# Places of their own for the first four steps of an attention and SoLU kernel, and two buffers for the keys

## The chip, the cores and the metric

One core of a Trainium2 chip. Its engines each run their own instructions in order: PE (TensorE, matrix products), DVE (VectorE), ACT (ScalarE), POOL (GpSimd), and SP (SyncE), which here only issues DMAs. The metric is the device time of one execution in microseconds (us); lower is better.

## What is computed

```python
scores = scale * np.matmul(q, k.transpose(0, 1, 3, 2))      # q, k, v: (8, 8, 576, 64)
kth = np.partition(scores, -32, axis=-1)[..., -32:-31]
scores = np.where(scores >= kth, scores, -1e9)
attn = np.exp(scores - scores.max(-1, keepdims=True))
attn = attn / (attn.sum(-1, keepdims=True) + 1e-09)
x = np.matmul(attn, v)                  # then heads side by side: (4608, 512)

h = x @ w_in                            # (4608, 1024)
solu = h * softmax(h)
ln = (solu - mean) / np.sqrt(var + 1e-06) * g_ln
out = ln @ w_out                        # (4608, 512)
```

The weights w_in and w_out come as 64-bit floats and are turned into 32-bit ones on the chip.

## The kernel before

**Work.** The 8 batches have 8 heads each, taken as 4 pairs of heads. A *step* is one of 32 equal pieces of the attention: four chunks of 128 queries, two from each of two head pairs, and one set of 64 last queries of one pair. With two heads per chunk that gives nine score tiles of 128 x 576 per step (`NT` = 9, index j). Four steps make a batch. After a half of a batch has its attention output (xT), the tokens pass the second part in groups of 128 (*token groups*: mm1, hexp, solu, square, ln, transposes, mm2, store), 36 groups in all.

**What one step does**, with the engine. SP loads the queries (`load_q`, L739), and for each head pair the keys with the last 64 queries and keys (`load_k`, L653) and the values (`load_v`). PE transposes queries (`prep_q`), keys (`prep_k`) and the last rows (`prep_t`); ACT copies them out of PSUM (`prep_qc`, `prep_kc`, `prep_tc`). PE forms products of keys with keys (`moments`, copied by `moments_c`); `spread` (PE), `spread_v`, `spread_r` (DVE), `first_p` (POOL) and `first` (DVE) make from them a first guess of each row's threshold. PE makes the scores (`scores`, L844, two tiles per call), ACT takes them to SBUF as X (`evac`). Then the threshold is refined: `count0` (DVE) counts entries above the first guess, `second` moves the guess, `count1` (seven tiles on ACT, two on DVE) and `third` refine it, `count2` (ACT) gives signs, `side`, `nearest`, `best` and `kth` (DVE) find the 32nd value. `exps` (ACT), `keep` and `inverse` (DVE) and `norm` (POOL) make probabilities, which PE transposes (`transpose_p`), ACT copies (`copy_p`), and PE multiplies with the values (`attn_v`, copied by `copy_v`).

**Weights.** 16 chunks of 128 x 512, w_in in chunks 0 to 7 and w_out in 8 to 15. Each is loaded (`load_w`) and converted by `w_bits` (three DVE instructions, L589, L593, L597), `w_low` (ACT, L605), `w_mul` and `w_add` (POOL, L629, L632); w_out also gets `w_gain`. At the end all chunks are read once more (`w_again`, `w_exp`, `w_check`) for a check of their range.

**Order.** It is written out by hand. Each call is put on a list with a planned time (`at`, L1173), from tables: `step_times` for a step (times from the step's own start, steps 39 apart), `key_times` for the four head pairs of a batch, `first_times` for the four token groups of the first batch, `token_times` and `tails_times` for the others, `last_times` for the last three, `weights_times` for the weights. The list is sorted by time and issued:

```python
    with tc.manual_schedule(engines={E.PE, E.Activation, E.DVE, E.Pool}):
        for _, _, f, args in sorted(todo, key=lambda x: x[:2]):
            f(*args)
```

So the planned times only make an order on PE, ACT, DVE and POOL; each instruction still waits for its data. SP is not in that set: its DMAs are put in order when the program is built, and each waits until its buffer is free.

**Buffers.** Pools `p1`, `p2`, `small`, `p8` hold 1, 2, 3 and 8 buffers of each tag. Keys (`km`, L658), the last queries and keys (`qt`, `kt`) and the step's queries (`qm`) have one buffer, raw weights two, X eight of two tiles each. In PSUM there are two buffers each for the scores (shared with `spread` and mm1), for transposes, and for the outputs (shared with `moments` and `prep_t`).

Of the kernel before, what the change touches and what calls it, by code (L numbers as in the profile page):

```python
# [15 lines left out]
P = 128  # L16
# [427 lines left out]
def fast_path(  # L444
# [23 lines left out]

    nc = tc.nc
# [3 lines left out]
    NM = 4  # L473
# [26 lines left out]

    pairs = [(b, hp) for b in range(B) for hp in range(NP)]
    steps = []
    for b in range(B):
        for half in range(2):
            for n in range(NP // 2):
                two = (2 * n + half, 2 * n + 1 - half)
                chunks = [(hp, 2 * half + t) for hp in two for t in range(2)]
                steps.append((b, chunks, two[0]))
# [144 lines left out]
    def load_k(n):  # L653
        b, hp = pairs[n]
        hh = slice(2 * hp, 2 * hp + 2)
        d = ks[n]

        d["k"] = p1.tile([P, 2 * NM, D], F32, tag="km", name="km")  # L658
        nc.sync.dma_start(
            out=d["k"].rearrange("p (t h) d -> p t h d", h=2),  # L660
            in_=k[b, hh, 0:SM, :].rearrange("h (p t) d -> p t h d", t=NM),
        )
        for nm, src in (("q", q), ("k", k)):
            d[nm + "t"] = p1.tile([ST, 2, D], F32, tag=nm + "t", name=nm + "t")
            nc.sync.dma_start(out=d[nm + "t"], in_=src[b, hh, SM:S, :].rearrange("h p d -> p h d"))
# [73 lines left out]
    def load_q(i):  # L739
        b, chunks, x = steps[i]  # L740
        d = st[i]
        d["q"] = p1.tile([P, NT, D], F32, tag="qm", name="qm")
        for c, (hp, t) in enumerate(chunks):
            nc.sync.dma_start(
                out=d["q"][:, 2 * c : 2 * c + 2, :],
                in_=q[b, 2 * hp : 2 * hp + 2, 0:SM, :].rearrange("h (p t) d -> p t h d", t=NM)[
                    :, t, :, :
                ],
            )
        for h in range(2):  # L750
            nc.sync.dma_start(
                out=d["q"][h * ST : (h + 1) * ST, 2 * NM, :], in_=q[b, 2 * x + h, SM:S, :]
            )

    def keys_of(i, c):

        b, chunks, x = steps[i]
        return ks[NP * b + (x if c == NM else chunks[c][0])]
# [217 lines left out]
    def kth(i):  # L976

        d = st[i]
        far = d["far"]
        hot = small.tile([P, NT, 8], F32, tag="hot", name="hot")  # L980
        nc.vector.tensor_tensor(
            out=hot, in0=ranks, in1=far.unsqueeze(2).broadcast_to([P, NT, 8]), op=ALU.is_equal
        )
        nc.vector.tensor_tensor(out=hot, in0=hot, in1=d["w8"].rearrange("p (t e) -> p t e", e=8), op=ALU.mult)
        zk = zk_all[:, i, :]
        nc.vector.tensor_reduce(out=zk, in_=hot, axis=AX.X, op=ALU.add)
        kt = small.tile([P, NT], F32, tag="kth", name="kth")
        nc.vector.tensor_tensor(out=kt, in0=d["al"], in1=zk, op=ALU.subtract)
        nc.vector.scalar_tensor_tensor(
            out=kt, in0=kt, scalar=-1.0, in1=kt, op0=ALU.mult, op1=ALU.max  # L990
        )
        d["kth"] = kt
# [72 lines left out]

    def attn_v(i, part):
        o = st[i]["om", part] = ps_o.tile([P, 512], F32, tag="o", name="om")
        n = 2 * P if part else SP
        vm, vt = keys_of(i, 2 * part)["v"]
        pt = pt_of(i, part)[:, :, 0:n]  # L1070

        for c in range(NM + 1):
            for h in range(2):
                hd = slice(h * ST, (h + 1) * ST)
                nc.tensor.matmul(  # L1075
                    out=o[h * D : (h + 1) * D, 0:n],
                    lhsT=vm[:, h, c, :] if c < NM else vt[hd, :],
                    rhs=pt[:, h * NM + c, :] if c < NM else pt[hd, 2 * NM, :],
                    start=(c == 0), stop=(c == NM),
                )  # L1080

    def copy_v(i, part):
        b, chunks, x = steps[i]
        hp, t = chunks[2 * part]
        o = st[i]["om", part]
        m = once(xs, ("m", b, t // 2), lambda: p2.tile([P, NP, 2 * P], F32, tag="xTm", name="xTm"))
        nc.scalar.copy(out=m[:, hp, :], in_=o[:, 0 : 2 * P])  # L1087
        if part == 0:
            m = once(xs, ("t", b // 2), lambda: p2.tile([P, NP, 2 * ST], F32, tag="xTt", name="xTt"))
            c = b % 2 * ST  # L1090
            nc.scalar.copy(out=m[:, hp, c : c + ST], in_=o[:, 2 * P : SP])
# [81 lines left out]
    def at(time, f, *args):  # L1173
# [38 lines left out]

    key_times = [
        (load_k, [-71.77, -54.35, -34.54, -26.23]),
        (load_v, [46.71, 33.98, 89.74, 55.28]),
        (prep_t, [-50.7, -40.81, -7.18, 29.61]),
        (prep_tc, [-44.69, -33.63, -1.87, 33.99]),
        (prep_k, [-57.81, -29.05, -14.02, 12.97]),
        (prep_kc, [-52.21, -21.98, -13.67, 19.04]),
        (moments, [-60.64, -32.24, -4.08, 14.96]),  # L1220
        (moments_c, [-42.18, -31.04, 2.87, 15.92]),
# [4 lines left out]
            (mm1, range(2), [55.33, 58.94]),  # L1226
            (hexp, [()], [62.09]),
            (solu, [()], [64.78]),
            (square, [()], [72.74]),
            (ln, [()], [74.12]),  # L1230
            (transpose_ln, range(2), [79.17, 82.08]),
            (copy_ln, range(2), [80.82, 83.25]),
            (mm2, range(2), [105.32, 109.34]),
            (store, [()], [116.42]),
        ],
        [
            (mm1, range(2), [56.02, 57.57]),
            (hexp, [()], [62.06]),
            (solu, [()], [63.63]),
            (square, [()], [64.41]),  # L1240
            (ln, [()], [70.76]),
            (transpose_ln, range(2), [71.53, 73.02]),
            (copy_ln, range(2), [73.11, 76.23]),
            (mm2, range(2), [103.2, 105.01]),
            (store, [()], [111.83]),
        ],
        [
            (mm1, range(2), [60.01, 58.42]),
            (hexp, [()], [60.84]),
            (solu, [()], [63.82]),  # L1250
            (square, [()], [66.16]),
            (ln, [()], [68.8]),
            (transpose_ln, range(2), [73.91, 72.15]),
            (copy_ln, range(2), [76.72, 73.77]),
            (mm2, range(2), [104.21, 109.94]),
            (store, [()], [122.21]),
        ],
        [
            (mm1, range(2), [56.27, 58.65]),
            (hexp, [()], [60.21]),  # L1260
            (solu, [()], [62.66]),
            (square, [()], [65]),
            (ln, [()], [71.02]),
            (transpose_ln, range(2), [72.95, 75.51]),
            (copy_ln, range(2), [75.72, 78.13]),
            (mm2, range(2), [100.81, 108.54]),
            (store, [()], [114.07]),
# [25 lines left out]
        (mm1, range(2), [67.83, 66.88]),  # L1293
        (hexp, [()], [71.58]),
        (solu, [()], [78.17]),
        (square, [()], [78.26]),
        (ln, [()], [85.86]),
        (transpose_ln, range(2), [91.97, 93.22]),
        (copy_ln, range(2), [93.92, 104.78]),
        (mm2, range(2), [103.52, 117.24]),  # L1300
        (store, [()], [177.72]),
# [4 lines left out]
            -179.04, -126.3, -52.39, -38.25, -33.45, 2.48, 8.22, 5.52, 52.89, 51.11, 62.18,  # L1306
            83.53, 63.6, 105.69, 111.2, 108.65,
        ]),
        (w_bits, w_wide, range(NW), [
            -155, -52.03, -42.38, -5.42, 15.63, 19.48, 57.75, 77.84, 84.56, 85.78, 92.26,  # L1310
            104.44, 115.57, 124.08, 129.87, 135.07,
        ]),
        (w_low, w_wide, range(NW), [
            -109.8, -76.02, -28.31, 1.47, 11.32, 38.79, 64.91, 76.6, 83.01, 89.83, 92.36,
            105.31, 118.79, 123.48, 128.94, 132.88,
        ]),
        (w_mul, w_wide, range(NW), [
            -73.72, -18.25, -6.71, 5.55, 20.66, 39.9, 66.53, 78.79, 93.74, 96.71, 105.83,
            111.35, 121.8, 126.63, 134.57, 135.6,
        ]),  # L1320
        (w_add, w_wide, range(NW), [
            -33.83, -13.24, 1.26, 14.88, 23.19, 58.85, 72.52, 85.73, 95.1, 99.85, 106.84,
            115.23, 122.2, 127.79, 135.39, 137.44,
        ]),
        (w_gain, True, range(8, NW), [
            113.17, 161.51, 144.58, 163.9, 157.15, 174.79, 165.41, 184.77,
        ]),
        (w_again, w_wide, range(NW), [
            1258.52, 1267.59, 1233.32, 1272.03, 1265.86, 1232.82, 1276.98, 1238.37, 1336.4,
            1328.98, 1268.82, 1395.91, 1275.47, 1295.42, 1317.39, 1347.09,  # L1330
        ]),
        (w_exp, w_wide, range(NW), [
            1333.3, 1343.97, 1271.41, 1284.48, 1356.37, 1274.22, 1344.94, 1304.11, 1362.07,
            1390.72, 1361.14, 1452.18, 1376.66, 1376.2, 1365.1, 1423.75,
        ]),
        (w_check, w_wide, range(NW), [
            1340.79, 1345.85, 1277.65, 1332.62, 1371.59, 1301.74, 1366.88, 1327.12, 1416.86,
            1444.15, 1370.39, 1493.58, 1432.99, 1419.36, 1417.83, 1433.7,
        ]),
    ]  # L1340

    at(-287.72, load_g)
    for f, needed, chunks, times in weights_times:
        for n, time in zip(chunks, times):
            if needed:
                at(time, f, n)
# [6 lines left out]
    for i in range(NSTEP):  # L1353
        all_times(i * STEP, step_times, i)
    for n in range(len(pairs)):
        for f, times in key_times:
            at(n // NP * NP * STEP + times[n % NP], f, n)
# [94 lines left out]
```

## Time and profile before

| | |
|---|---|
| median of 3 runs | 1300.66 us (1299.98 to 1301.05) |
| the profiled execution | 1299.98 us |
| its span, first to last instruction | 1298.1 us |
| busy: PE, DVE, ACT, POOL | 1194.8, 1154.8, 1118.8, 479.6 us |
| mean granted TensorE clock | 0.963 |
| 16 DMA engines, share of the span | 16% |

Busy time is the sum over an engine's instructions; with shares of 92, 89 and 86% no engine stands out, so the question is where in the span each is idle. In the lines shown later, a row of a timeline begins with its start and its duration in us, then engine, line of the kernel, operation, output tile and inputs, and in brackets the idle time of the engine before it and what ended it. A row of stretches begins with the stretch and its length, then the busy time of PE, of PE's weight loads, of DVE, ACT and POOL (number of instructions in brackets), the granted clock (1.00 is full), the mean busy share of the DMA engines, and GB/s.

### The profile page before, as it was taken

What the parts mean: (1) busy time and instruction counts of PE and PEld (TensorE: products, weight loads), DVE (VectorE), ACT (ScalarE), POOL (GpSimd) and SP (SyncE); (2) the same over time, 40 slices, a digit from 0 to 9 for tenths busy, and PEclk for the clock granted to TensorE, in tenths of its full rate; (3) what the DMA queues carried; (4) which work ended last, traced back from release to release, by engine and by line L of the source; (5) the groups of instructions that cost most, each with busy time, mean ns of one, the idle gap of its engine ahead of it and who ended that gap; (6) DMA issues with size and microseconds to landing.
All of it is one profiled execution on the core that took longest, in us unless ns stands there. A gap on an engine that the chain in (4) does not pass through costs nothing.

```text
span 1298.1 us, 20306 instructions
## 1 busy us (share of the span) xinstructions
PE 1194.8 (92%) x6243; PEld 658.0 (51%) x6243; DVE 1154.8 (89%) x2974; ACT 1118.8 (86%) x2446; POOL 479.6 (37%) x583
## 2 busy tenths in 40 slices
PE   5645879999999999999999999999999999998996
PEld 3323445555555555555555555555555555554543
DVE  4899999999999997999999997999999997999612
ACT  3787889999999889999999889999999889999534
POOL 4244654443333234443333244443333234443310
PEclk9666889999999999999999999999999999999999
DMA  6212211101110111101210112111210111102421
GB/s 163 81 43 61 67 38 28 37 22 37 46 36 17 30 32 50 34 23 31 54 36 18 30 30 54 28 29 30 55 35 19 31 28 43 30 9 73 130 73 44
DMA packets 106246, 57.00 MB, mean 44 GB/s; under 512 B 89224, under 2 KB 97424, under 8 KB 106128
## 3 DMA queue, kind: packets, MB, share of 16 engines
q1 hardware_dynamic: 106128, 55.61, 15.7%
q8 instruction: 52, 0.85, 0.3%
q14 instruction: 66, 0.54, 0.1%
HBM read 46.14 MB, written 9.44 MB: 43 GB/s over the span
## 4 chain that ended last, share of the span: by engine, by line
PE 59%; ACT 18%; DVE 15%; issue 3%; POOL 3%; DMA 1%; SPq 0%; DVEq 0%; POOLq 0%; ACTq 0%
PE o_ps L1157 15%; PE s_ps L858 12%; PE h_ps L1099 12%; PE tp_p L1026 7%; PE om L1075 7%; DVE junkv L875 4%; ACT junka L897 4%; DVE E L997 3%; ACT sg L932 3%; ACT PT L1038 2%; PE tp_ln L1146 2%; ACT E L968 2%; DVE w L953 2%; DVE w L960 2%; ACT X L867 2%
## 5 line engine op out<-in xcount | busy, mean ns | idle before, releaser
L1157 PE MATMUL o_ps<-w_out,lnT 128*128 128x512 f32 x576 | 261.8, 598 | 0.2 <-ACT osb L1164 0.2
L875 DVE TENSOR_SCALAR_CACHE_REDUCE junkv<-X,t 128x576 bf16<-128x576 f32 x288 | 230.7, 801 | 11.9 <-ACT X L867 7.3
L1012 POOL TENSOR_SCALAR E<-E,rden 128x576 f32<-128x576 f32 x256 | 204.7, 813 | 87.0 <-DVE rden L1008 76.5
L925 POOL TENSOR_SCALAR tt<-t 128x9 f32<-128x9 f32 x32 | 21.8, 680 | 573.3 <-DVE t L919 573.3
L1099 PE MATMUL h_ps<-w_in,xTm 128*128 128x512 f32 x512 | 226.7, 595 | 0.3 <-ACT xTm L1087 0.3
L953 DVE SCALAR_TENSOR_TENSOR w<-X,al,sg 128x576 f32<-128x576 f32 x256 | 210.6, 824 | 0.1
L960 DVE MAX8 w<-w 128x8 f32<-128x576 f32 x288 | 210.5, 749 | 0.0
L997 DVE SCALAR_TENSOR_TENSOR E<-X,kth,E 128x576 f32<-128x576 f32 x256 | 200.0, 818 | 9.7 <-ACT E L968 9.6
L858 PE MATMUL s_ps<-kT,qT 64*128 64x288 f32 x1024 | 195.7, 458 | 5.5 <-ACT X L867 4.5
L932 ACT ACTIVATE sg<-X,t 128x576 bf16<-128x576 f32 x256 | 195.6, 768 | 2.8 <-DVE t L919 2.8
L897 ACT ACTIVATE junka<-X,t 128x576 bf16<-128x576 f32 x224 | 174.3, 778 | 19.4 <-DVE t L888 15.6
L867 ACT ACTIVATE X<-s_ps 128x576 f32<-128x576 f32 x256 | 157.2, 655 | 36.0 <-PE s_ps L858 32.4
L1026 PE MATMUL tp_p<-ident,E 128*128 128x128 f32 x1024 | 155.5, 285 | 26.4 <-POOL E L1012 21.6
L1026 PEld LDWEIGHTS tp_p<-ident,E 128*128 128x128 f32 x1024 | 116.0, 144 | 92.9 <-issue 37.5
L1038 ACT COPY PT<-tp_p 128x512 f32<-128x512 f32 x256 | 145.6, 595 | 19.5 <-PE tp_p L1026 19.3
L1157 PEld LDWEIGHTS o_ps<-w_out,lnT 128*128 128x128 f32 x576 | 104.3, 190 | 110.6 <-issue 107.8
L1099 PEld LDWEIGHTS h_ps<-w_in,xTm 128*128 128x128 f32 x512 | 94.6, 190 | 109.7 <-issue 102.4
L968 ACT ACTIVATE E<-X 128x1152 f32<-128x1152 f32 x128 | 146.5, 1174 | 0.0
L1075 PE MATMUL om<-PT,vm 128*64 128x256 f32 (+1 forms) x1024 | 140.0, 416 | 0.0
L858 PEld LDWEIGHTS s_ps<-kT,qT 64*128 64x128 f32 x1024 | 116.2, 199 | 46.7 <-ACT X L867 18.1
L1075 PEld LDWEIGHTS om<-PT,vm 128*64 128x64 f32 x1024 | 68.5, 138 | 59.7 <-issue 22.5
L818 POOL TENSOR_TENSOR zs<-zs,phalf 128x9 f32<-128x9 f32 x32 | 70.2, 2194 | 2.7
(127 smaller groups left out, 1631.8 us busy)
## 6 DMA issues: line engine op xcount, KB each, us to landing
km<-in_k_dram SPq DMA_DIRECT2D x32, 256.0 KB, 3.3
qm<-in_q_dram SPq DMA_DIRECT2D x128, 64.0 KB, 2.1
vm<-in_v_dram SPq DMA_DIRECT2D x32, 256.0 KB, 2.8
out_dram<-osb SPq DMA_DIRECT2D x32, 256.0 KB, 2.3
w_raw<-in_moe_w_in_dram SPq DMA_DIRECT2D x8, 512.0 KB, 4.4
w_raw<-in_moe_w_out_dram SPq DMA_DIRECT2D x8, 512.0 KB, 3.3
w_again<-in_moe_w_in_dram SPq DMA_DIRECT2D x8, 512.0 KB, 4.6
w_again<-in_moe_w_out_dram SPq DMA_DIRECT2D x8, 512.0 KB, 4.1
```

The costliest lines, as they stand in the source:

```text
L858: nc.tensor.matmul(out=s[:, half, 0:SH], lhsT=queries_of(i, t)[hd, :], rhs=kT[hd, k0 : k0 + SH], start=True, stop=True,)
L875: nc.vector.tensor_scalar(out=junk, in0=x_of(i, j), scalar1=st[i][t][:, j : j + 1], scalar2=None, op0=ALU.is_ge, op1=ALU.add, accum_out=co ...
L897: nc.scalar.activation(out=junk, in_=x_of(i, j), func=AF.Sign, scale=-1.0, bias=d["t1"][:, j : j + 1], accum_out=columns(i, "n1")[:, j : j ...
L932: nc.scalar.activation(out=d["sg", j], in_=x_of(i, j), func=AF.Sign, scale=-(1.0 + 2.0**-23), bias=d["t2"][:, j : j + 1], accum_out=column ...
L953: nc.vector.scalar_tensor_tensor(out=w, in0=x_of(i, j), scalar=d["al"][:, j : j + 1], in1=d.pop(("sg", j)), op0=ALU.subtract, op1=ALU.mult,)
L960: nc.vector.max(w8[:, j, :], st[i].pop(("w", j)))
L997: nc.vector.scalar_tensor_tensor(out=e, in0=x_of(i, j), scalar=d["kth"][:, j : j + 1], in1=e, op0=ALU.is_ge, op1=ALU.mult, accum_out=den_a ...
L1012: nc.gpsimd.tensor_scalar(out=e, in0=e, scalar1=st[i]["rden"][:, j : j + 1], scalar2=1.0, op0=ALU.mult, op1=ALU.mult,)
L1026: nc.tensor.transpose(tp[:, c, :], e[:, c * P : (c + 1) * P], ident)
L1075: nc.tensor.matmul(out=o[h * D : (h + 1) * D, 0:n], lhsT=vm[:, h, c, :] if c < NM else vt[hd, :], rhs=pt[:, h * NM + c, :] if c < NM else ...
L1099: nc.tensor.matmul(out=h[:, half, :], lhsT=x[:, c, :], rhs=w_in[:, c, half * 512 : (half + 1) * 512], start=(c == 0), stop=(c == NP - 1),)
L1157: nc.tensor.matmul(out=o, lhsT=d["lnT"][:, c, :], rhs=w_out[:, c, :], start=(c == 0), stop=(c == NF - 1),)
```

## The change

Steps 0 to 3, the first four head pairs, the four token groups of the first batch, the last three token groups and the weights get new planned times. Steps 4 to 31 and later keys keep theirs. Keys get a second buffer; `hot`, a small tile of `kth`, goes from three buffers to one. The list of steps is written in another way, and `attn_v` and `copy_v` go over runs of columns that belong to one head pair.

```diff
-        for half in range(2):
-            for n in range(NP // 2):
-                two = (2 * n + half, 2 * n + 1 - half)
-                chunks = [(hp, 2 * half + t) for hp in two for t in range(2)]
-                steps.append((b, chunks, two[0]))
+        for t in range(NM):
+            two = (t % 2 * 2 + t // 2, t % 2 * 2 + 1 - t // 2)
+            steps.append((b, [(hp, t // 2 * 2 + n) for hp in two for n in range(2)]))
...
-        d["k"] = p1.tile([P, 2 * NM, D], F32, tag="km", name="km")
+        d["k"] = p2.tile([P, 2 * NM, D], F32, tag="km", name="km")
...
-        hot = small.tile([P, NT, 8], F32, tag="hot", name="hot")
+        hot = p1.tile([P, NT, 8], F32, tag="hot", name="hot")
...
+    def runs_of(i, part):
+        chunks = steps[i][1]
+        n, end = 2 * part, SP if part == 0 else 2 * P
+        if chunks[n][0] == chunks[n + 1][0]:
+            return [(n, slice(0, end))]
+        return [(n, slice(0, P)), (n + 1, slice(P, end))]
...
     def attn_v(i, part):
...
+        for n, cols in runs_of(i, part):
+            vm, vt = keys_of(i, n)["v"]
+            pt = pt_of(i, part)[:, :, cols]
...
+    early_times = [
+        [
+            (load_q, [()], [-61.79]),
+            (prep_q, [()], [-36.38]),
+            (prep_qc, [()], [-19.65]),
+            (spread, [()], [-15.66]),
...
+            (scores, range(5), [-12.59, -9.08, -6.79, -4.4, 4.25]),
+            (evac, range(9), [-10.34, -9.57, -7.99, -5.62, -0.77, -0.44, 2.85, 4.16, 4.43]),
...
+            (exps, range(5), [50.66, 51.48, 60.18, 53.95, 50.04]),
...
     key_times = [
-        (load_k, [-71.77, -54.35, -34.54, -26.23]),
+        (load_k, [-166.62, -49.24, -48.06, -20.27], [-71.77, -54.35, -34.54, -26.23]),
...
-        (moments, [-60.64, -32.24, -4.08, 14.96]),
+        (moments, [-121.41, -34.78, -17.44, 10.53], [-60.64, -32.24, -4.08, 14.96]),
...
     last_times = [
-        (mm1, range(2), [67.83, 66.88]),
+        (mm1, range(2), [63.43, 54.45]),
...
     for i in range(NSTEP):
-        all_times(i * STEP, step_times, i)
+        all_times(i * STEP, early_times[i] if i < len(early_times) else step_times, i)
     for n in range(len(pairs)):
-        for f, times in key_times:
-            at(n // NP * NP * STEP + times[n % NP], f, n)
+        for f, first, later in key_times:
+            at(n // NP * NP * STEP + (later if n >= NP else first)[n % NP], f, n)
```

(The first rows of `early_times` are step 0's, the row of exps shown last is step 3's.) Sorted by planned time, the first calls stand in this order on each engine; the number in round brackets is the step, head pair or weight chunk, and where a step has tiles or score calls, the step is in square brackets and these in round ones.

| | before | after |
|---|---|---|
| SP, as in the built program | g, w(0,1), km, qt and kt(0), qm(0), km, qt and kt(1), w(2,3), qt(2), km(2), kt(2), w(4), qm(1) | w(0), g, km, qt and kt(0), w(1), qm(0), km, qt and kt(1), km, qt and kt(2), w(2,3), qm(1) |
| PE | moments(0), prep_k(0), prep_t(0), prep_t(1), moments(1), prep_k(1), prep_q(0), spread(0), prep_k(2), scores\[0\](0) | moments(0), prep_k(0), prep_t(0), prep_q(0), moments(1), prep_t(1), prep_k(1), moments(2), spread(0), scores\[0\](0) |
| ACT | w_low(0,1), prep_kc(0), prep_tc(0), moments_c(0), prep_tc(1), moments_c(1), w_low(2), prep_kc(1), prep_qc(0), prep_kc(2), evac\[0\](0 to 3) | w_low(0,1), prep_kc(0), moments_c(1), prep_tc(0,1), prep_qc(0), moments_c(0), prep_kc(1), evac\[0\](0,1), prep_kc(2), evac\[0\](2,3), w_low(2) |
| DVE | w_bits(0,1,2), spread_v(0), spread_r(0), w_bits(3), first(0), count0\[0\], second(0), w_bits(4) | w_bits(0,1), spread_v(0), spread_r(0), w_bits(2), first(0), w_bits(3), count0\[0\], second(0), w_bits(4) |
| ACT, after step 0's count1 | prep_qc(1), prep_kc(3), count2\[0\] (eight tiles), prep_tc(3), evac\[1\] | evac\[1\](1,0), count2\[0\] (five tiles), evac\[1\](2,3), then both in turn |
| DVE, from kth(2) to the first inverse | kth(2), count1\[3\](8), keep\[2\] three times, third(3), keep\[2\] three times, inverse | kth(2), third(3), keep\[2\] five times, inverse |
| ACT, near step 5's spread | prep_qc(5), exps\[3\](3,4), prep_kc(7) | prep_qc(5), prep_kc(7), exps\[3\](2) |
| PE, after the last attn_v | half of an mm2, mm1, half of an mm2, mm1 | mm1, half of an mm2, half of an mm1, half of an mm2 |

(g is g_ln; w(n) is the load of weight chunk n; km, qt and kt are the three DMAs of load_k; qm those of load_q.) The tables of weights and of the first batch's token groups have new numbers of the same kind, not shown.

## Prediction

> **What bounds the kernel now.** I read the forty slices first (rows: tenths of each slice in which an engine is busy, and the granted TensorE clock), then the stretches, then single waits in order of time.
>
> ```profile
> PE   5645879999999999999999999999999999998996
> DVE  4899999999999997999999997999999997999612
> PEclk9666889999999999999999999999999999999999
> ```
>
> PE is full from the eighth slice to the last but one; only the first seven are loose. VectorE is full from the third slice on. Four stretches (busy us per engine, then clock, DMA share, GB/s) say it in numbers:
>
> ```profile
> 0.00:58.00 58.00, 32.63 (x152) 21.07 (x154) 34.51 (x81) 31.16 (x75) 19.32 (x36) 0.84 0.50 128
> 58.00:170.00 112.00, 65.26 (x349) 36.71 (x345) 109.68 (x256) 84.71 (x184) 55.73 (x51) 0.71 0.18 54
> 170.00:1236.40 1066.40, 1045.49 (x5606) 576.47 (x5606) 997.37 (x2600) 979.28 (x2137) 398.78 (x488) 1.00 0.14 37
> 1236.40:1298.10 61.70, 51.47 (x140) 23.71 (x138) 13.22 (x39) 23.69 (x53) 5.83 (x9) 0.95 0.19 62
> ```
>
> So: until 58 us nobody is full (VectorE idle 23.5); from 58 to 170 VectorE is the bound (109.7 of 112) and PE waits; from 170 on PE is the bound. The hand-over is one wait, the first transposes of step 2's probabilities, and a smaller one follows:
>
> ```profile
> 170.14 1.11 PE L1026 MATMUL tp_p<-ident,E 128*128 128x128 f32 x4 [7.21 <-POOL E L1012]
> ...
> 204.15 0.24 PE L780 MATMUL y_ps<-mom,qT 64*128 64x65 bf16 x4 [1.97 <-ACT kT L718]
> ```
>
> What PE has to do from 170.14 on is fixed, so the end moves by as much as that wait ends earlier. What sets it is VectorE's start:
>
> ```profile
> 16.05 0.43 DVE L589 TENSOR_SCALAR w_tmp<-w_raw 128x512 uint32<-128x512 uint32 x1 [5.82 <-DMA w_raw<-in_moe_w_in_dram]
> ...
> 18.44 0.69 DVE L798 TENSOR_TENSOR yq<-y_ps,qm 128x512 f32<-128x512 f32 x1 [0.78 <-PE y_ps L780]
> ...
> 36.20 0.17 DVE L886 TENSOR_TENSOR u<-c,tb 128x9 f32<-128x9 f32 x1
> ...
> 42.97 0.24 DVE L909 SCALAR_TENSOR_TENSOR step<-n,tb 128x7 f32<-128x7 f32 x2 [1.26 <-ACT junka L897]
> ...
> 71.14 0.22 DVE L981 TENSOR_TENSOR hot<-ranks,far 128x72 f32<-128x72 f32 x1
> ```
>
> These are, in order: the third weight chunk, spread_v of step 0, the end of step 0's first counts (second), the end of its second counts (third), and its kth.
>
> **The edits with no price.** The rewritten list of steps holds the same 32 steps, and both pairs of chunks of a part share a head pair, so `runs_of` returns one run and attn_v and copy_v emit the same instructions as before. `hot` in one buffer is written and read only by VectorE, in order: no wait. Steps 4 to 31 keep their places. Every engine has the same instructions; only orders move: the start, and the end.
>
> **The start, step by step.** In the old order PE had prep_t(1), which waits for qt(1) (landed at 13.13), then moments(1) and prep_k(1), ahead of prep_q(0), and ScalarE had w_low(2) ahead of step 0's copies: it ran at 16.03, when chunk 2 landed, and qT was copied after it, at 17.17; spread(0) started at 17.81. Now prep_q(0) follows prep_t(0), and w_low(2) stands behind four of step 0's evacuations. With two key buffers SP issues km(1) straight after the queries, near 8.5 instead of 9.49, and km(2) near 10.5 instead of 15.67, since it no longer waits for PE to finish with km(1). But qt and kt keep one buffer: on SP, qt(2), kt(2), chunks 2 and 3 and the queries of step 1 stay queued behind PE's prep_t(1). And moments(1) and moments(2) now stand ahead of spread(0), so it waits for km(2). km(0) took 5.9 us from issue to landing while the weights moved, km(2) of before 3.5 (15.67 to 19.2); with 4 it lands at 14.5, and after ScalarE's moments_c, prep_tc, prep_qc and prep_kc (0.2, 0.5, 0.5, 0.6 in the rows) spread(0) starts at 16.0: 1.8 earlier.
>
> Chunk 3's w_bits (1.5) now stands between first(0) and the counts, so they start at 23.1 against 23.28; but PE and ScalarE make the scores 1.8 earlier meanwhile. Before, the counts waited 1.2 us for each of five evacuations (3.1 us apart, the last ending at 35.3); that chain should end near 32.4, and second(0) comes at 34.2, not 36.2. ScalarE's seven counts at 0.9 and qT's copy at 0.5 put third(0) at 41.5 to 41.6 instead of 42.97. Then evacuations of step 1 lie between step 0's count2, so VectorE has step 1's counts between nearest and best: I find no gap after side(1), at 45.4 instead of 46.37. From there to kth(0) both orders hold the same calls less spread_r(1) and chunk 6 (2.2 us), which now fill the wait before side(1): the row's 24.7 us less those and its 0.9 of gaps is 21.6, kth(0) at 67.0. **Gain there: 4.1 us.**
>
> **The full stretch.** Price VectorE's calls by start to start in rows without gaps: count 0.73 (0.21 more if a count follows), nearest 0.73, best 0.67, keep 0.74, w_bits 1.53, kth 1.07, spread_v 0.88, spread_r 0.67, third 0.65, inverse 0.38, solu 1.75, second 0.40, first 0.35, side 0.18. One late step sums to 35.0, and the kth of late steps start 35.0 apart, so the list holds. Before, kth(0) to the first norm of step 2 (168.9) sums to 87.6 and took 97.8: 10.2 lost. Now the list is 86.8, since one keep and one count fewer stand before the first inverse: 0.8 gained. On the other side ScalarE has to wait for scores of step 2 before count2[1], and I see about 0.8 of VectorE waiting on it near 81. These cancel.
>
> Here a rule speaks against counting any of it as gain. The 10.2 lost are rows like
>
> ```profile
> 124.51 1.37 DVE L597 TENSOR_SCALAR w_tmp<-w_tmp 128x512 uint32<-128x512 uint32 x1
> ```
>
> which takes 0.43 alone, while POOL runs w_low and E. The Trainium skill (SBUF — State Buffer, Who interferes with whom) says that VectorE and GpSimd share one port pair under an exclusive lock, so that the loser stands still for the other's whole instruction. The change moves these POOL operations about but removes none: nine chunks' mul and add (18 at 1.27 us, a row) still fall into this stretch, 22.9 us if each blocked, 10.2 by the row. I keep the row's 10.2; the ends are nothing lost and 22.9.
>
> **PE after the wait.** The rule on the clock (TensorE: Matmul & The Clock Gate, What's actually happening) starts a matmul stretch at half rate after an idle window; the row agrees in kind (scores at 172.57 took 2.37, at 246.01 1.24). A shorter wait would have to vanish to save the warming, worth at most the 2.8 us that a granted clock of 0.72 cost from 170 to 180; the new order keeps an idle stretch there, so I count none of it. At 204.15 PE waited 1.97 for kT, because ScalarE ran two exps (1.6) between qT and kT; the new order puts prep_kc(7) right behind prep_qc(5): 1.5 gained (bounds 0 and 2.6).
>
> **The end.** After the last attn_v PE has 51.4 us of matmuls and no gap above 0.2. Before, a ready mm2 half came first; now mm1, which needs the last xT copy (0.37): 0.5 lost (bounds 0 and 2, for a re-read weight chunk that lands late ahead of a solu). The close after it (store, last check, branch: 1287.8 to 1298.1) keeps its order.
>
> **Sum:** -4.1 - 0.8 + 0.8 - 1.5 + 0.5 = -5.1 against the profiled execution's own 1299.98 (span 1298.1 and 1.88 around it): 1294.9. The median of the runs is 0.68 above that one, so **1295.6 us**.
>
> **Rivals.**
> - *More comes back* (0.20). The lost 10.2 shrink to half because adds and norms of POOL fall beside VectorE work with one operand in SBUF (best, and the counts that lost nothing in the rows): another 5.1, so 1290.5. For it: loss is a matter of meeting, not of amount. Against: the same number of operations in the same stretch.
> - *The start is hidden* (0.17). VectorE comes 4 us earlier, but ScalarE (35.3 of 40 us busy between 170 and 210) or a late chunk of weights holds step 2's keeps, and PE's wait ends as before: only the 1.5 less 0.5 remain, 1299.7. Against: ScalarE was busy only 84.7 of 112 in the VectorE stretch.
> - *The third keys hold the first spread* (0.12): slower. moments(2) is in front of spread(0) on PE, and behind it stand step 0's scores, ScalarE's evacuations and every count. Each us that km(2) lands after 17.9 is lost beyond the old time, less the 1.0 of the later gains. Landing at 22, 7.5 later than I take, it costs 4.1 - 1.0 = 3.1: 1303.8. For it: the DMA engines were 0.76 busy from 10 to 20, and km(0) took 5.9. Against: km(2) now stands before chunks 2 and 3.
>
> That the change does nothing is excluded: the orders of all engines differ.
>
> **How the numbers follow.** The forecast has 0.51. Its own bounds (start 2 to 6, wait 0 to 2.6, end 0 to 2) give 1291 to 1299. The range reaches up to 1301.5, over the hidden case, and down to 1289, past the larger gain; about 0.08 stays below and 0.12 above. A measurement here tells 0.2% (2.6 us) from no change: faster means below 1298.06. Forecast (0.47 of its 0.51), the larger gain (0.20) and little of the hidden case (0.05) make 0.72; the rest of those two and a little of the slow one make 0.17 same; 0.11 slower.
>
> **What would show it.** spread(0) near 16.0, second(0) near 34.2, kth(0) near 67, kth of step 1 and 2 about 4 earlier, then 35.0 apart; PE's wait before step 2's transposes ending near 166; no wait for kT at step 5's spread; 51 to 52 us from the last attn_v to PE's end. A spread(0) after 17.8, or a kth(0) at 67 with step 2's transposes at 170, would make it wrong.

## The result and the profile after

| | before | after |
|---|---|---|
| median of 4 runs each, on one chip, us | 1300.86 | 1289.32 |
| range of these runs | 1299.98 to 1301.14 | 1288.38 to 1291.58 |
| the profiled execution | 1299.98 | 1291.58 |
| its span | 1298.1 | 1289.7 |

The ratio is 0.9915, with a 95% interval of 0.9898 to 0.9932: 11.5 us less, where 5.1 were forecast. The direction is right and the time lies inside the range; the size is not. The profiled run of after is the slowest of its four and that of before the quickest, so the two traces differ by 8.4 us only. The other 3.1 are in no trace here.

The forty slices of after (tenths of busy time, and the granted TensorE clock):

```profile
PE   7577799999999999999999999999999999998996
DVE  5999989999999988999999988999999998999512
PEclk9567889999999999999999999999999999999998
```

The stretches of after (length, then busy us and instructions of PE, its weight loads, VectorE, ScalarE and GpSimd, then clock, DMA share, GB/s):

```profile
0.00:58.00 58.00, 39.81 (x169) 22.34 (x169) 40.17 (x96) 36.33 (x83) 23.29 (x39) 0.79 0.52 143
58.00:170.00 112.00, 78.75 (x384) 44.86 (x384) 108.77 (x274) 88.72 (x194) 64.72 (x61) 0.71 0.19 54
170.00:1226.00 1056.00, 1035.55 (x5546) 568.03 (x5546) 986.92 (x2568) 971.03 (x2119) 387.35 (x475) 1.00 0.14 37
1226.00:1289.70 63.70, 52.38 (x150) 23.92 (x146) 12.09 (x38) 23.42 (x51) 5.82 (x9) 0.95 0.15 51
```

VectorE issues 96 instructions before 58 us instead of 81, and 274 instead of 256 in the next 112 us, in less busy time (108.8 against 109.7). So it started sooner, and in the full stretch an instruction took less time on average. Since nothing was removed, the second is what needs explaining.

The single steps, from the timeline of after (start, duration, engine, line, tiles, and in brackets the idle time ahead of it):

```profile
13.22 0.42 PE L729 MATMUL pre<-km 128*64 128x64 bf16 x8
13.58 0.29 PE L780 MATMUL y_ps<-mom,qT 64*128 64x65 bf16 x4
...
14.59 0.69 DVE L798 TENSOR_TENSOR yq<-y_ps,qm 128x512 f32<-128x512 f32 x1 [4.05 <-PE y_ps L780]
...
31.77 0.17 DVE L886 TENSOR_TENSOR u<-c,tb 128x9 f32<-128x9 f32 x1
...
63.46 0.21 DVE L981 TENSOR_TENSOR hot<-ranks,far 128x72 f32<-128x72 f32 x1
...
156.79 1.38 PE L1026 MATMUL tp_p<-ident,E 128*128 128x128 f32 x8 [0.57 <-POOL E L1012]
```

These are moments(2), which waited for nothing, and right behind it spread(0); spread_v(0), second(0), kth(0), and the first transposes of step 2. Put beside the trace of before, with the kth of the later steps and the end of the last attn_v:

| us | before | after | shift |
|---|---|---|---|
| spread(0) | 17.81 | 13.58 | -4.2 |
| second(0) | 36.20 | 31.77 | -4.4 |
| kth(0) | 71.14 | 63.46 | -7.7 |
| kth(1) | 114.56 | 104.14 | -10.4 |
| kth(2) | 160.36 | 149.73 | -10.6 |
| transposes of step 2 | 170.14 | 156.79 | -13.4 |
| kth(3) | 198.13 | 188.66 | -9.5 |
| kth(5) | 268.14 | 258.84 | -9.3 |
| last attn_v ends | 1236.5 | 1227.3 | -9.2 |

The lead grows to 7.7 us by kth(0), to 10.6 by kth(2), stands at 13.4 for a moment on TensorE, and falls back to 9.3. From there on it stays between 8.5 and 10.0.

### The profile page after: what moved, and what is told of

Read it like the earlier page. It is cut to its first block, busy times and chain, and to the rows that moved or that the text cites. A ratio compares the mean times of both kernels' runs of the same rounds, so it can differ in the third digit from the quotient of the medians.

```text
span 1289.7 us, 20290 instructions
## 1 busy us (share of the span) xinstructions
PE 1206.5 (94%) x6243; PEld 659.2 (51%) x6243; DVE 1147.9 (89%) x2974; ACT 1119.5 (87%) x2446; POOL 481.2 (37%) x583
## 4 chain that ended last, share of the span: by engine, by line
PE 58%; ACT 19%; DVE 18%; issue 3%; SPq 0%; POOL 0%; DMA 0%; DVEq 0%; ACTq 0%; POOLq 0%
PE o_ps L1170 14%; PE h_ps L1112 12%; PE s_ps L858 12%; PE tp_p L1026 7%; PE om L1083 7%; DVE junkv L875 4%; DVE E L997 4%; ACT junka L897 4%; ACT sg L932 3%; DVE w L960 3%; DVE w L953 3%; ACT E L968 2%; ACT PT L1038 2%; PE tp_ln L1159 2%; ACT X L867 2%
## 5 line engine op out<-in xcount | busy, mean ns | idle before, releaser
L1112 PE MATMUL h_ps<-w_in,xTm 128*128 128x512 f32 x512 | 229.5, 600 | 6.7 <-ACT xTm L1098 6.7
L858 PE MATMUL s_ps<-kT,qT 64*128 64x288 f32 x1024 | 203.3, 465 | 7.8 <-ACT X L867 6.2
L997 DVE SCALAR_TENSOR_TENSOR E<-X,kth,E 128x576 f32<-128x576 f32 x256 | 199.5, 816 | 10.4 <-ACT E L968 10.0
L897 ACT ACTIVATE junka<-X,t 128x576 bf16<-128x576 f32 x224 | 174.7, 780 | 15.1 <-DVE t L888 11.5
```

The source lines that it names most:

```text
L858: nc.tensor.matmul(out=s[:, half, 0:SH], lhsT=queries_of(i, t)[hd, :], rhs=kT[hd, k0 : k0 + SH], start=True, stop=True,)
L897: nc.scalar.activation(out=junk, in_=x_of(i, j), func=AF.Sign, scale=-1.0, bias=d["t1"][:, j : j + 1], accum_out=columns(i, "n1")[:, j : j ...
L997: nc.vector.scalar_tensor_tensor(out=e, in0=x_of(i, j), scalar=d["kth"][:, j : j + 1], in1=e, op0=ALU.is_ge, op1=ALU.mult, accum_out=den_a ...
L1112: nc.tensor.matmul(out=h[:, half, :], lhsT=x[:, c, :], rhs=w_in[:, c, half * 512 : (half + 1) * 512], start=(c == 0), stop=(c == NP - 1),)
```

## The experiments

Three questions came out of this table. Is the start really set by the loads and the second key buffer? Does VectorE lose less to GpSimd than before? And why does TensorE give 4 us back after step 2's transposes? Each time below is a median with its ratio to runs of before on the same chip (their medians: 1299.5 to 1299.8); the milestones are from the run's own profile.

### The second buffer for keys, taken back

```diff
-        d["k"] = p2.tile([P, 2 * NM, D], F32, tag="km", name="km")
+        d["k"] = p1.tile([P, 2 * NM, D], F32, tag="km", name="km")
```

> The kernel after with one buffer for keys instead of two. Theory A (the second buffer and the early loads set spread(0) at 13.6): km(2) is issued only after prep_k(1) has read km(1), near 13.3 us, and lands near 16.7; spread(0) comes near 17.2, kth(0) near 67, and the time is 3 to 3.6 us above the kernel after, about 1292.7. Theory B (the early orders alone do it, km(2) has slack): spread(0) at 13.6 to 14.2 and 1289.3, no change.

1293.55 us, ratio 0.9957 (0.9943 to 0.9971). TensorE's rows in its timeline:

```profile
17.04 0.43 PE L729 MATMUL pre<-km 128*64 128x64 bf16 x8 [3.59 <-DMA km<-in_k_dram]
17.40 0.40 PE L780 MATMUL y_ps<-mom,qT 64*128 64x65 bf16 x8
```

moments(2) now waits 3.59 us for km(2), and spread(0), behind it on TensorE, comes at 17.40 instead of 13.58. kth(0) is 3.2 later, the last attn_v 2.7, the median 4.2. Theory A holds. In the new order a late start is passed on almost whole.

### The buffer alone, in the old order

The same line in the kernel before, with hot in one buffer to make room.

> The kernel before with two buffers for keys (and hot in one buffer, to make room), all places old. Theory A (buffers and places count only together): km(1) still stands behind the queries, and its prep behind prep_t(1), so spread(0) within 0.5 of 17.8 and the time within 1 us of 1299.5 to 1300.9. Theory B (the buffer alone lets km(2) and what is queued behind it on SP go 2 to 3 us earlier, which the counts feel): 1297 to 1298.5.

1301.71 us, ratio 1.0011 (0.9998 to 1.0024); spread(0) at 17.27, kth(0) at 72.02. Theory A: without the new places the second buffer buys nothing.

### Weight chunk 1 ahead of the first keys

```diff
         (load_w, True, range(NW), [
-            -265.85, -158.41, -39.22, ...
+            -265.85, -170.41, -39.22, ...
```

> The kernel after with one load moved: weight chunk 1 again ahead of km(0), as before the change. Theory A (km(0) behind only one chunk is what brings spread(0) forward): moments(0) 1.9 us later, at 8.0, spread(0) near 15.4, kth(0) and the end 1.5 to 1.9 later, about 1291. Theory B (spread(0) hangs on km(1) and km(2), issued at 7.6 and 9.8 either way): moments(0) later, but spread(0) within 0.4 of 13.6 and the time unchanged, 1289.3.

1291.56 us, ratio 0.9942 (0.9921 to 0.9964). moments(0) came 2.7 us later and spread(0) at 15.61, so that part of A is right. But kth(0) was only 1.2 later, kth(3) 0.2, and the last attn_v ended at 1227.25, as in after. The median is 2.2 above after's and the profiled span 0.1 below it: whether the end felt it stays open. In the trace the delay shrank where TensorE had more clock than in after: the first full-rate stretch on record began at 22.9 us instead of 30.0, and second(0) was only 0.7 later; from 160 to 170 us the clock was 1.00 instead of 0.50, and the 1.9 us that were left at kth(2) were 0.2 at kth(3). The clock is taken up again below.

### The end in its old places

last_times, w_again, w_exp and w_check as in the kernel before.

> The kernel after with the old places at the end (last token tiles, re-reads of the weights). Theory A (trace of after: 51.0 instead of 51.4 from the last attn_v to PE's end): 0.4 slower, 1289.7. Theory B (as forecast, mm1 first costs 0.5): 0.5 faster, 1288.8. Either way the milestones up to the last attn_v stay within 0.5 us, and all but 1 us of the change's 11.5 is there without the new end.

1289.36 us, ratio 0.9920 (0.9897 to 0.9943), against after's 1289.32. The new end is worth nothing that these runs can tell.

### GpSimd's part of the widening left out, in both kernels

```diff
-        val, power = tmp[:, 0, :].bitcast(U32), tmp[:, 1, :].bitcast(U32)
+        val, power = w_chunks[n][0].bitcast(U32), tmp[:, 1, :].bitcast(U32)
...
     def w_mul(n):
-        nc.gpsimd.tensor_tensor(out=low, in0=low, in1=w_tmp[n][:, 1, :], op=ALU.mult)
+        pass
```

and the same for w_add.

> The kernel before without GpSimd's part of the widening: VectorE writes the upper word straight into the weight tile, w_mul and w_add are left out (32 operations of 1.27 us), so the weights lose their low bits; VectorE's and ScalarE's instructions stay. Theory A (VectorE loses time to these operations between kth(0) and kth(3): 11.7 us over the sum of its list): at least 6 of the 11.7 come back, kth(0) to kth(3) takes 121 us or less instead of 127.0, time 1289 to 1294. Theory B (the loss has another source, or E's norms on GpSimd alone make it): kth(0) to kth(3) within 2 us of 127.0, time 1298 to 1300.

> The kernel after, w_mul and w_add left out in the same way. Theory A (the change had already avoided about half of that loss): only 3 to 4 us come back between kth(0) and kth(2), 86.3 in after, 83 here, and the time is 1286 to 1288; the distance to the kernel before, both without these operations, is then 5 to 8 us instead of 11.5. Theory B: kth(0) to kth(2) within 1 us of 86.3, and the distance stays 11.5.

The kernel before falls to 1289.19 us, ratio 0.9921 (0.9901 to 0.9940); after to 1286.00, ratio 0.9893 (0.9877 to 0.9910). kth(0) and kth(3) in the timeline of before without these operations:

```profile
66.94 0.21 DVE L978 TENSOR_TENSOR hot<-ranks,far 128x72 f32<-128x72 f32 x1
...
185.57 0.21 DVE L978 TENSOR_TENSOR hot<-ranks,far 128x72 f32<-128x72 f32 x1
```

and of after without them:

```profile
62.96 0.22 DVE L978 TENSOR_TENSOR hot<-ranks,far 128x72 f32<-128x72 f32 x1
...
184.62 0.23 DVE L978 TENSOR_TENSOR hot<-ranks,far 128x72 f32<-128x72 f32 x1
```

From kth(0) to kth(3) VectorE needs 118.6 us instead of 127.0 in the old order, and 121.7 instead of 125.2 in the new one. So w_mul and w_add cost VectorE 8.4 us there before and 3.5 after. Theory A holds in both, and more strongly than I had written: without these operations the medians of the two kernels are 3.2 us apart, not 5 to 8. (That distance is rough: the four runs of the kernel before without them are two near 1287.6 and two near 1290.7. Some of the 4.2 us by which the first kth(0) is earlier than before's 71.14 has another cause, told at the end; the stretch behind it has no wait in VectorE's rows.) The same stretch as a row, for before, after, before without the two operations and after without them:

```profile
71.14:198.13 126.99, 87.63 (x495) 51.40 (x496) 124.47 (x291) 98.19 (x215) 67.95 (x69) 0.76 0.19 55
63.46:188.66 125.20, 96.39 (x481) 54.45 (x482) 119.29 (x298) 102.17 (x224) 69.43 (x67) 0.77 0.17 50
66.94:185.57 118.63, 86.41 (x495) 50.11 (x496) 116.11 (x290) 97.61 (x214) 38.96 (x49) 0.80 0.21 59
62.96:184.62 121.66, 95.42 (x481) 53.53 (x482) 115.55 (x297) 101.42 (x224) 41.97 (x48) 0.77 0.18 51
```

VectorE's busy time (the third of the five) falls by 8.4 us in the old order and by 3.7 in the new one, and its idle time hardly moves (2.5 and 2.5, 5.9 and 6.1). So what went away is longer instructions, not waits for a shorter GpSimd queue.

It isn't that fewer of them fall there. GpSimd's busy time in w_mul and then in w_add, in the stretch from kth(0) to kth(3), before:

```profile
71.14:198.13 126.99, 14.02 (x10) 0.76 0.19 55
...
71.14:198.13 126.99, 13.55 (x10) 0.76 0.19 55
```

and after:

```profile
63.46:188.66 125.20, 12.77 (x9) 0.77 0.17 50
...
63.46:188.66 125.20, 14.62 (x10) 0.77 0.17 50
```

27.6 us before and 27.4 after: the same amount, of which VectorE lost 30% in the one order and 13% in the other. What changed is beside which VectorE instruction each of them falls. In before a w_add met an instruction on two small tiles (of `second`), which takes 0.17 us alone and here ended together with the w_add:

```profile
106.26 1.27 POOL L632 TENSOR_TENSOR w_out<-w_tmp,w_low 128x512 f32<-128x512 f32 x1
...
106.31 1.24 DVE L888 TENSOR_TENSOR t<-u,ta 128x9 f32<-128x9 f32 x1
```

In after one met `best` (MAX8) and a count, which each read one large tile and took what they take alone:

```profile
98.06 1.27 POOL L632 TENSOR_TENSOR w_out<-w_tmp,w_low 128x512 f32<-128x512 f32 x1
...
98.16 0.75 DVE L960 MAX8 w<-w 128x8 f32<-128x576 f32 x1
98.83 0.79 DVE L875 TENSOR_SCALAR_CACHE_REDUCE junkv<-Xt,t 128x576 bf16<-128x576 f32 x1
```

That holds for all of them: 23 counts and MAX8 met a w_mul or w_add in this stretch of before and 29 in after, and none took more than 0.81 us. By the starts and durations of the rows, w_mul and w_add ran beside such instructions for 13.1 us before and 17.9 after, and beside VectorE's other instructions for 15.7 us before and 10.8 after. The second pair is 4.9 us apart, as the two losses are (8.4 and 3.5).

### The front of the change alone

```diff
-        all_times(i * STEP, early_times[i] if i < len(early_times) else step_times, i)
+        all_times(i * STEP, early_times[i] if i < 1 else step_times, i)
```

in the kernel after; chunks 7 to 15, w_gain, the token tiles and the end get their old times, and prep_tc(3) 33.99 instead of 36.73, which the old order of step 1 needs. What is left of the change are two key buffers and the places of step 0, of the first keys and of chunks 0 to 6.

> Of the change only the front: two key buffers, the places of step 0, of the keys of the first batch and of weight chunks 0 to 6; steps 1 to 3, token tiles, chunks 7 to 15 and the end at their old places. Theory A (start and the meeting of VectorE with GpSimd are two separate gains): spread(0) near 13.6, kth(0) near 66 (list 47.1 before it, against 46.1 in after), kth(0) to kth(3) again about 126 to 127 with 8 us lost to GpSimd, last attn_v and time 4 to 5 us under before, near 1295.5. Theory B (the front alone brings the loss down too, because everything behind it meets differently): 1290 to 1292. Theory C (nothing without the places behind it): 1299.

1297.65 us, ratio 0.9987 (0.9976 to 0.9998). spread(0) at 13.39 and kth(0) at 65.23, 5.9 before the old one; but kth(1) leads by 2.9, kth(3) by 3.6 and the last attn_v by 2.1. Less reached the end than theory A had: a new wait ate 2.7 of it. VectorE's row in the timeline:

```profile
85.36 0.17 DVE L828 TENSOR_TENSOR t<-mean,zs 128x9 f32<-128x9 f32 x1 [2.66 <-POOL zs L818]
```

and GpSimd's rows ahead of it:

```profile
79.46 1.96 POOL L1012 TENSOR_SCALAR E<-E,rden 128x576 f32<-128x576 f32 x2 [0.33 <-DVE rden L1008]
81.39 1.76 POOL L632 TENSOR_TENSOR w_in<-w_tmp,w_low 128x512 f32<-128x512 f32 x1
83.24 0.20 POOL L814 TENSOR_SCALAR zs<-ss 128x9 f32<-128x9 f32 x1
83.52 1.80 POOL L818 TENSOR_TENSOR zs<-zs,phalf 128x9 f32<-128x9 f32 x1
```

VectorE needs zs at 82.7; in GpSimd's queue a w_add stands ahead of it, whose 1.76 us are the larger part of the 2.66. Here a lead given to VectorE was lost in part because GpSimd's queue still held the old order.

### The front alone, without w_mul and w_add

The edits of the last two sections together.

> The run front_only with w_mul and w_add left out as in nopool_before and nopool_after. Theory A (the places of steps 1 to 3, of the token tiles and of the later weights are worth only the avoided meeting of VectorE with these GpSimd operations, and the start's lead only reaches the end where GpSimd is out of the way): kth(0) to kth(3) near 119 to 120 instead of 129.3, time within 1.5 us of nopool_after, 1286 to 1287.5. Theory B (those places are worth something by themselves, such as the filled waits): kth(0) to kth(3) 122 or more, time 1289 or more.

1288.85 us, ratio 0.9909 (0.9892 to 0.9927); kth(0) to kth(3) in 120.8 us. It falls between the two theories. The stretch loses 8.5 of the 129.3 us that it took with them, nearly as A has it, but the time stays 2.9 above that of the kernel after without them (1286.00). No run of the one is as low as a run of the other (1286.58 to 1289.18, and 1285.92 to 1286.41), so some of the places behind the front seem to be worth something by themselves; which ones wasn't tried. Against the kernel before without these operations (1289.19) the front gains 0.3 us, which is nothing that these runs can tell: that its lead reaches the end once GpSimd is out of the way, as theory A also had it, isn't seen.

### Steps 1 to 3 in the general table, and the token tiles too

The edit of all_times shown for the front alone and its prep_tc(3), with all else as in after; in the second run the token tiles of the first batch at their old times as well.

> The kernel after with steps 1 to 3 back in the general table (and prep_tc of key pair 3 at its old place, which their order needs); step 0, keys, weights and token tiles as in after. Theory A (the places of steps 1 to 3 bring VectorE 3 us between kth(0) and kth(2), by meeting fewer POOL operations and by spread_r(1) and step 1's counts filling waits): kth(0) 1 to 2 later, kth(2) 4 to 5 later than in after, time 1292.5 to 1294. Theory B (the whole gain is step 0, keys and weights): within 1 us of 1289.3. Theory C (the places of steps 1 to 3 cause what is given back after step 2's transposes): faster, 1287.

> The run steps123_old with the token tiles of the first batch at their old places as well. Theory A (its 21 us came from token tiles placed for other steps: TensorE did their mm2 ahead of the scores of step 5, and VectorE waited 6.2 us for X): that wait is gone, 1294 to 1298. Theory B (the places of the later weight chunks do not fit the old steps): still above 1303.

1310.24 us, ratio 1.0081 (1.0056 to 1.0106), and with old token tiles 1305.5, ratio 1.0046 (1.0027 to 1.0064). Both are slower than the kernel before, which none of the three theories of the first run had. VectorE's waits for X between kth(3) and kth(4) are 6.2 us in the first and 3.4 in the second: the token tiles are a part of the cause, but the time is that of theory B. The second run differs from the front alone only in the places of chunks 7 to 15 (with w_gain) and the end, and the end was worth nothing in the kernel after: so the new places of these chunks cost some 7.9 us beside old steps. These tables pay only together.

### Five idle matmuls ahead of the first mm1

```diff
+        if half == 0 and d["tag"] == 0:
+            for _ in range(5):
+                nc.tensor.matmul(
+                    out=h[:, 0, :], lhsT=ident, rhs=w_in[:, 0, 0:512], start=True, stop=True
+                )
```

This run is about the 4 us given back. In after TensorE waits 5.85 us for xTm, until 148.52; the clock is granted at half rate from 146.1 to 152.9 and, after 6.8 us at full rate, again from 159.7 to 170.0. The scores of step 4 in its timeline:

```profile
162.56 2.52 PE L858 MATMUL s_ps<-kT,qT 64*128 64x288 f32 x8
...
165.59 2.83 PE L858 MATMUL s_ps<-kT,qT 64*128 64x288 f32 x8
...
170.15 1.24 PE L858 MATMUL s_ps<-kT,qT 64*128 64x288 f32 x8
```

Eight take 2.5 to 2.8 us there and 1.24 once the clock is up. VectorE's counts wait for the last of them:

```profile
177.09 0.81 DVE L875 TENSOR_SCALAR_CACHE_REDUCE junkv<-Xt,t 128x576 bf16<-128x576 f32 x1 [2.30 <-ACT Xt L867]
```

> The kernel after with five matmuls more, ahead of the first mm1, into the PSUM tile that it then overwrites: they fill some 5 of the 5.9 us in which TensorE waits there for xTm, and feed nothing. Theory A (the half clock granted from 160 to 170 makes step 4's scores late, VectorE waits 2.3 us for Xt, and this gives 2 us back): the clock from 150 to 170 is 0.9 or more, the wait for Xt falls under 0.5, kth(3) comes near 186.7 and the time is near 1287.3. Theory B (the give-back is ScalarE's, which is full from 170 to 200): clock up, but kth(3) within 0.5 of 188.7 and 1289.3. Theory C (TensorE is only delayed): kth(3) later, 1291.

1291.33 us, ratio 0.9936 (0.9919 to 0.9953). The stretches 160 to 170 and 190 to 200 of this run:

```profile
160.00:170.00 10.00, 8.93 (x57) 5.72 (x55) 9.46 (x24) 7.51 (x17) 9.45 (x12) 0.83 0.28 63
...
190.00:200.00 10.00, 8.21 (x27) 4.30 (x27) 9.63 (x27) 8.66 (x23) 6.23 (x6) 0.70 0.27 67
```

and VectorE's waits in its timeline:

```profile
175.29 0.81 DVE L875 TENSOR_SCALAR_CACHE_REDUCE junkv<-Xt,t 128x576 bf16<-128x576 f32 x1 [1.27 <-ACT Xt L867]
...
211.07 0.81 DVE L875 TENSOR_SCALAR_CACHE_REDUCE junkv<-X,t 128x576 bf16<-128x576 f32 x1 [2.06 <-ACT X L867]
```

kth(3) comes at 186.85, 1.8 earlier, as theory A had it: the half clock does delay step 4's scores. The rest of theory A failed: the wait is 1.27, not under 0.5, and the time is no better. The low stretch of the clock moved on (0.70 from 190 to 200, where after had 1.00), VectorE now waits 2.06 for step 5's X, kth(4) is 0.7 later than in after, and the last attn_v ends at 1227.7. The gain lived for some 25 us. Why the clock is lowered again after 159.7 in after, with TensorE busy for 8.7 of the 10 us before, stays open.

### Fifteen idle matmuls at the very start

```diff
+    at(-300.0, warm, 15)
     at(-235.01, load_g)
```

where warm multiplies ident by ident into the PSUM tile of key pair 0.

> The kernel after with 15 matmuls of ident by ident more, in the 4 us in which TensorE has nothing to do at the start (into the PSUM tile of key pair 0, which is then overwritten). Theory A (the first scores run at a lowered clock because TensorE stood idle: 8 of them took 2.3 to 3.5 us in after, 1.8 in the run nopool_before, whose counts ended 4 us earlier): scores of step 0 at 1.8 or less, second(0) 2 to 3 us earlier, 1287. Theory B (so short a stretch of work does not change the clock 10 us later): second(0) within 0.5 of 31.8 and 1289.3.

1292.0 us, ratio 0.9950 (0.9931 to 0.9968). The rows of TensorE:

```profile
1.76 6.49 PE L726 MATMUL pre<-ident 128*128 128x128 f32 x30 [1.76 <-POOL ident masks.py:199]
...
16.59 3.47 PE L863 MATMUL s_ps<-kT,qT 64*128 64x288 f32 x8
```

Each matmul was two passes, so they ran until 8.2 and held moments(0) back by 2.2 us: spread(0) at 16.07, kth(0) 1.7 later. And the first scores were as slow as in after (3.47 us for eight), behind a wait of 2.3 us. By the clock's record they did bring it to full rate, but only from 7.8 to 14.6 us: it was back at half when the first scores started at 16.59. Theory B, with a loss that neither theory had.

## Why the prediction was wrong in size

**Two steps failed. The one whose mechanism was wrong is in the full stretch: "I keep the row's 10.2."** The forecast took the time that VectorE loses to GpSimd as the same in both orders, since the same operations stay in the stretch. The pair of runs without w_mul and w_add showed 8.4 us of loss before and 3.5 after. By the forecast's prices, the calls from kth(0) to kth(3) sum to 115.3 us in the old order and 117.3 in the new one, and took 127.0 and 125.2. So 11.7 were lost before (the 10.2 of the forecast end at step 2's first norm, 30 us sooner). Of the 7.9 after, 3.0 are waits for ScalarE (0.36, 0.32 and 2.30 in VectorE's rows), and 4.9 are left as loss. That is 6.8 less; the runs without w_mul and w_add account for 4.9 of it, and the other 2 or so lie in what remains above the list without them (3.3 us before, 1.2 after), which no run takes apart. The rival "more comes back" had the mechanism, with 5.1 for its size. The page that was weighed there (the Trainium skill, SBUF — State Buffer, Who interferes with whom) says that only some VectorE instructions share the port pair, those with two SBUF inputs among them. The rows agree: counts and MAX8 lost nothing, and an instruction on two small tiles took 1.24 us for 0.17. Both orders hold the same instructions but for one count and one `third` more in the new one, and the loss more than halved: beside which one an operation falls is what the forecast should have counted. It counted operations.

The second failed step is the start, a term of the right kind and the wrong size. The other terms, with it, in the order of the sum:

- **Start, forecast -4.1, measured -7.7 at kth(0).** The mechanism was right, the size was 3.6 us short. spread(0) was put at 16.0 and came at 13.58, for two reasons that the old rows and the order of the loads could have given. km(0) now stands ahead of weight chunk 1, so moments(0) ran at 6.09 instead of 7.99; I had moved only km(1) and km(2). And km(2), issued at 9.76, was there by 13.22, 3.5 us later, where I took 10.5 and 4. From spread(0) on the distances are the old ones (18.2 to second(0), before 18.4), and what lies between side(1) and kth(0) took 21.2, for which 21.6 was forecast.
- **A wait of 0.8 near 81: not there.** No row of VectorE between kth(0) and kth(2) shows a wait.
- **"The end moves by as much as that wait ends earlier": wrong.** The transposes of step 2 came 13.4 us earlier and the last attn_v 9.2. TensorE was no longer the bound at once: from 156.8 to 200 it was granted 0.88 of its clock (in the stretch of the same length before, from 170.1, it was 0.94), which is 2.6 us of 43.2, and idle for 1.0 us more (4.3 against 3.2): by this estimate 3.6 of the 4.1 to 4.2. Late scores of step 4 made VectorE wait, too, so kth(3) leads by 9.5 only. This is what the forecast's words on the clock had left at nothing.
- **The wait for kT, forecast -1.5: gone, and worth nothing.** spread(5) ran at 189.28 without a wait; 5 us later TensorE waited 1.80 us for E of step 3 instead.
- **The end, forecast +0.5: 0.** From the last attn_v to TensorE's end 51.0 us instead of 51.4, and the run with the old end has the same median.

The start's 3.6 us are the larger miss of the two at the milestones. As a sum over the two traces: -7.7 to kth(0); then +2.0 of calls, -6.8 of loss and +3.0 of waits to kth(3), together -1.8; +0.2 from there to the last attn_v; +0.8 at the end, where what follows TensorE's last matmul of the second part took 1.2 us longer in this execution. But for rounding that is the 8.4 of the spans. Against the forecast's terms, the start brought 3.6 us more and the full stretch 1.8 more, since 2.0 of calls and 3.0 of waits stood against the 6.8 that were no longer lost; kT, the end and the rest brought about 2 less. The medians, 11.5 apart, say more for the loss: 3.2 are left without w_mul and w_add.

**"The start is hidden" was partly true.** The front alone reaches the end with 2.1 us of the 5.9 that it has at kth(0). In the whole change the start is passed on (one buffer less costs 4.2), as far as the runs tell because the other queues were moved with it. So start and loss are not two terms that can be added; the forecast treated them so. **"The third keys hold the first spread"** did not happen: moments(2) waited for nothing. The run with one buffer shows that it does happen, with 3.59 us, as soon as km(2) is issued 4 us later.

Two small readings of the forecast were off, and nothing hangs on them: TensorE's row stands at 9 from the seventh slice on, not the eighth, and the old counts waited for four evacuations (1.2 to 1.4 us each), not five.

## What to carry to other kernels

Where two engines disturb each other, price the pairs that an order brings together, not the operations that it contains: here the same 27 us of GpSimd cost 8.4 us in one order and 3.5 in another. When the bound is about to pass from one engine to the next, a wait that vanishes is worth no more than what is late next, the clock of the waiting engine included. A table of places is one thing: here half of it was worth a fifth of the whole or, beside the wrong other half, less than nothing. In a start that is bound by loads, go through the load queue entry by entry, from its head.

## What was not expected of the hardware

In most runs the column of the granted clock says nothing of the first 20 to 35 us (in the run with the old end, of the first 82). It reads 1.00 ahead of the first stretch that the trace has on record. That first one is at full rate and begins at 35.6 us in before, at 30.0 in after, at 22.7 in before without w_mul and w_add. The first and the last of these both read 1.00 from 20 to 30 us, while eight score matmuls took, in the timeline of before,

```profile
26.38 2.74 PE L858 MATMUL s_ps<-kT,qT 64*128 64x288 f32 x8
```

and in that of the run without the two operations

```profile
25.16 1.77 PE L855 MATMUL s_ps<-kT,qT 64*128 64x288 f32 x8
```

A single one of them lasts 0.68 to 0.85 us in the first and 0.40 to 0.51 in the second. The same values stand in after at a recorded clock of 0.50 (162.56 us) and 1.00 (170.15), so before was still at half rate there. The front alone shows both in one trace, with full rate on record from 21.0 to 24.4 us and half from there to 31.2:

```profile
21.77 1.77 PE L858 MATMUL s_ps<-kT,qT 64*128 64x288 f32 x8 [0.59 <-ACT X L867]
23.82 2.83 PE L858 MATMUL s_ps<-kT,qT 64*128 64x288 f32 x8 [0.27 <-ACT X L867]
```

In before without the two operations, step 0's counts ended 4.1 us earlier (32.14 instead of 36.20) with the earlier rise. Why the clock rises when it does stays open: it was at 21.0 us in the front alone and at 29.7 in the same kernel without GpSimd's two operations, where the order on TensorE is the same.

And the clock's gain moves on: 4.5 us of matmuls that feed nothing kept it at 1.00 from 145 to 155, where after had 0.61 and 0.71, and after the wait of 2.73 us that TensorE then had ahead of step 2's transposes it was 0.65 from 155 to 160. These are one trace each.
